# The exponentials of a banded attention, turned by transposing DMA transfers instead of TensorE and VectorE

## The chip, the cores and the metric

The kernel runs on one core of one Trainium2 chip. Five engines have their own instruction streams: TensorE (PE) multiplies and transposes into PSUM, VectorE (DVE) and ScalarE (ACT) work element by element, GpSimd (POOL) does so without access to PSUM and issues loads, SyncE (SP) issues transfers. Sixteen DMA engines carry out the transfers of all queues. The metric is device time in microseconds (us) of one execution, the median of several; lower is better.

## The reference

An attention over chunks of 32 tokens comes first: each chunk sees 16 tokens to the left, itself, 8 to the right, and 8 memory tokens, 64 in all. Then each token goes to two of eight experts. Cut to what matters:

```python
batch, n_heads, seq, head_dim = (4, 8, 768, 64)          # chunk, left, right = 32, 16, 8
for c in range(seq // chunk):
    k_full = concat([mem_k, k_ctx]); v_full = concat([mem_v, v_ctx])
    scores = scale * q_c @ k_full.T
    a = exp(scores - max(scores)); a = a / (sum(a) + 1e-09)
    out[:, :, c_start:c_end] = a @ v_full
x = out.transpose(0, 2, 1, 3).reshape(3072, 512)
noisy = x @ w_gate + log1p(exp(x @ w_noise)) * noise     # 8 experts, the best two are kept
for e in range(8):
    h = maximum(x[mask] @ w1[e], 0.0)                    # 512 -> 1024 -> 512
    out[mask] += top2_w[mask, k, None] * (h @ w2[e])
```

## The kernel before

The attention is a loop over 16 units (`NPAIR`), the expert part follows. Two units make up a group of four heads of one batch entry; a unit is one half of the 768 tokens of four heads: 3 tiles of 128 tokens (`UB`), 12 chunks. The instructions of each engine run in the order in which they are written (a manual schedule), and the loop (lines 591 to 648) interleaves several units by hand. For unit n:

- `qkT_pe` (L265): TensorE transposes q and k, ScalarE copies them out (L268, and L276 in `kT_act`), two to three units ahead.
- `scores_pe` (L290, L300, L305): scores of four heads and three tiles into one PSUM tile `ps_s`, of which there is one buffer. The 64 keys of a chunk are kept as even and odd halves of 32 columns.
- `max_dve` (L313), then `sub_dve`: VectorE subtracts the maximum (L318), ScalarE takes the exponential into `P` (L320), bf16, 128 tokens x 6 blocks x 128 columns, two buffers. A block is one tile and one half of the keys; its 128 columns are four heads x 32 keys.
- `PT_pe` (L327): six transposes by TensorE, one for each block, into the PSUM tile `p_p`. `PT_dve` (L332): one VectorE copy into `PT`, two buffers, in SBUF.
- `PV_pe`: the six products with the memory values and a column of ones (L341), then 24 with the values of the chunks (L345), both with `PT` as the stationary operand, into `ps_o`.
- `mult_dve`: VectorE takes the reciprocals (L357) and writes the normalised rows to `xrow` (L358).
- `xT_pe` (L369, copied out in L371): transposes of these rows for the router. After every fourth unit the router of a batch entry begins (`begin_route`, L549 on), and its small steps are spread over the next units by `early_steps` and `late_steps`.

In turn i of the loop the order is: transposes of P(i-1); maximum of i; transposes of q and k for a later unit; router steps; copy of PT(i-1); subtraction and exponential of i; PV(i-1); scores of i+1; more router steps; multiplication of i-1; `xT_pe` of i-2; loads. So on TensorE PV(i-1) stands ahead of the scores of i+1, and on VectorE the multiplication of i-1 ahead of the maximum of i+1. The last unit's P is turned behind the loop (lines 649 to 655).

Three PSUM buffers (`psT`, tag "tr") serve the transposes of q and k, of P and of the rows, and the router.

GpSimd's queue issues the loads of q, k, v and of the expert weights (L126, L134, L538, L543). SyncE's queue has few transfers in this stage: the memory values (L164) at the start, the router's weights (L209) and the noise (L215) in turns 3, 6 and 10, and `write_rows` (L548), which writes a batch entry's rows to memory in router step s4, in turns 8 and 12 for the first two batch entries and near or behind the end of the loop for the others. A transfer on this queue waits in order for what it needs.

Of the kernel before, what the change touches and what calls it, by code (L numbers as in the profile page):

```python
# [13 lines left out]
BF16 = mybir.dt.bfloat16  # L14
# [10 lines left out]
def kernel(  # L25
# [14 lines left out]
    nc = tc.nc  # L40
# [19 lines left out]
    NPAIR = B * HP  # L60
# [38 lines left out]
    def body():  # L99
        actx = ExitStack()  # L100
        ap_ = actx.enter_context(tc.tile_pool(name="ap", bufs=2))
# [61 lines left out]
        for hd in range(2 * GP):  # L163
            nc.sync.dma_start(  # L164
                out=mv_nat[QW * hd + WP:QW * hd + QW].rearrange("p g e d -> p g (e d)"),
                in_=bass.AP(mem_v.tensor, mem_v.offset + hd * n_mem * D, [[2 * D, n_mem // 2], [2 * GP * n_mem * D, NG], [1, 2 * D]]))
# [88 lines left out]
        st = [dict() for _ in range(NPAIR)]  # L255
# [22 lines left out]
        UB = BT // 2  # L278
# [29 lines left out]
        def bc4(ap, n):  # L308
            return ap.rearrange("p h (u o) -> p h u o", o=1).to_broadcast([128, 2, BT, n])
# [6 lines left out]
        def sub_dve(n):  # L316
            sd = ap_.tile([128, 2, BT, CTX], F32, name="sd")
            nc.vector.tensor_tensor(out=sd, in0=st[n]["ps"], in1=bc4(st[n]["mx"], CTX), op=Alu.subtract)  # L318
            P = ap_.tile([128, 2 * UB, 4, QW], BF16, name="P")
            nc.scalar.activation(out=P.rearrange("p x h c -> p h x c"), in_=sd.rearrange("p x (h u) (e c) -> p (x h) (u e) c", h=2, e=2), func=Act.Exp, scale=scale)  # L320
            st[n]["P"] = P

        def PT_pe(n):
            P = st[n]["P"]
            p_p = psT.tile([128, 2 * UB, 128], BF16, name="p_p", tag="tr")
            for x in range(2 * UB):
                nc.tensor.transpose(out=p_p[:, x, :], in_=P[:, x, :, :], identity=identb)  # L327
            st[n]["p_p"] = p_p

        def PT_dve(n):  # L330
            PT = ap_.tile([128, 2 * UB, 128], BF16, name="PT")
            nc.vector.tensor_copy(PT, st[n]["p_p"])  # L332
            st[n]["PT"] = PT

        def PV_pe(n):
            g, half = divmod(n, 2)
            PT, vg = st[n]["PT"], groups[g][2]
            po = psO.tile([128, UB, 512], F32, name="ps_o")
            for u in range(UB):
                for e in range(2):  # L340
                    nc.tensor.matmul(out=po[:, u, :OW], lhsT=PT[:, 2 * u + e, :], rhs=memv[:, g, e, :], start=(e == 0), stop=False, skip_group_check=True)  # L341
            for x in range(CB):
                u, r = divmod(x, 4)
                for e in range(2):
                    nc.tensor.matmul(out=po[32 * r:32 * r + 32, u, :MD], lhsT=PT[:, 2 * u + e, 32 * r:32 * r + 32],  # L345
                                     rhs=vg[:, CB * half + x, :, e, :], start=False, stop=(e == 1), skip_group_check=True)
# [244 lines left out]
        for i in range(NPAIR):  # L591
            if i >= 1:
                PT_pe(i - 1)
# [7 lines left out]
            if i >= 1:  # L601
                PT_dve(i - 1)
# [42 lines left out]
            if i == GP * (NG - 3) + 1:  # L645
                load_w1(0)
                load_w2(0)
                load_w1(1)
        n = NPAIR - 1
        PT_pe(n)  # L650
        PT_dve(n)
        xT_pe(n - 1)
        late_steps()
# [223 lines left out]
        for e in range(E):  # L877
# [38 lines left out]
            if e == E - 1:  # L916
# [3 lines left out]
                    out=out_part[NB], out_offset=bass.IndirectOffsetOnAxis(ap=s_si[:, 0:1], axis=0),  # L920
                    in_=spart[:, 0, :], in_offset=None, bounds_check=N - 1, oob_is_err=False)
# [11 lines left out]
    with tc.For_i(SPILL, end, 128) as i:  # L933
# [7 lines left out]
        for t in range(NP):  # L941
# [11 lines left out]
            out=xl, out_offset=None, in_=xd, in_offset=bass.IndirectOffsetOnAxis(ap=gi[:, 0:1], axis=0),  # L953
# [10 lines left out]
        with tc.For_i(0, E, 1) as e:  # L964
# [17 lines left out]
            out=out, out_offset=bass.IndirectOffsetOnAxis(ap=si[:, 0:1], axis=0),  # L982
            in_=o, in_offset=None, bounds_check=N - 1, oob_is_err=False)
# [30 lines left out]
```

## Time and profile before

| | us |
|---|---|
| time, median of 3 runs | 334.02 (332.93 to 334.89) |
| time of the profiled execution | 335.33 |
| its span | 333.7 |
| TensorE busy in the span | 288.1 (86%) |
| VectorE, ScalarE, GpSimd busy | 169.9, 133.4, 138.6 |
| first and last start of a unit's maximum (L313) | 14.7, 94.3 |
| granted TensorE clock, mean over the span | 0.957 |

A row of a group gives its line, engine and operation, what it writes and reads, how many instructions, busy time and mean length of one, and the idle time of the engine in front of them with what ended it. A row of a timeline gives start, length and the same names; in brackets stands the idle time in front of it and what ended it. "PEld" is TensorE's loading of the stationary operand. A row of one line's or one tile's instructions has the shortest, median and longest duration in ns, then the first and the last start. "SPq" is SyncE's sequencer: the length there is how long the issue held it, not how long the data took. Rows of DMA queues give packets, MB and the time of their packets as a share of sixteen engines' span; it passes 100% where an engine has several packets in hand.

### The profile page before, as it was taken

What the parts mean: (1) busy time and instruction counts of PE and PEld (TensorE: products, weight loads), DVE (VectorE), ACT (ScalarE), POOL (GpSimd) and SP (SyncE); (2) the same over time, 40 slices, a digit from 0 to 9 for tenths busy, and PEclk for the clock granted to TensorE, in tenths of its full rate; (3) what the DMA queues carried; (4) which work ended last, traced back from release to release, by engine and by line L of the source; (5) the groups of instructions that cost most, each with busy time, mean ns of one, the idle gap of its engine ahead of it and who ended that gap; (6) DMA issues with size and microseconds to landing.
All of it is one profiled execution on the core that took longest, in us unless ns stands there. A gap on an engine that the chain in (4) does not pass through costs nothing.

```text
span 333.7 us, 7301 instructions
## 1 busy us (share of the span) xinstructions
PE 288.1 (86%) x3019; PEld 173.5 (52%) x3019; DVE 169.9 (51%) x343; ACT 133.4 (40%) x235; POOL 138.6 (42%) x181
## 2 busy tenths in 40 slices
PE   1697887977776377999999999999999999999990
PEld 0575675755654256554754754544544544544540
DVE  7789859849958775222322323424342433434451
ACT  7877788757433033533333332332303303202200
POOL 7877868538023472781008007007152042042152
PEclk9999999979989559999999999999999999999997
DMA  7999999999997136699407905914959624521031
GB/s 99 179 163 176 184 163 163 210 143 101 214 225 216 23 88 93 128 156 238 87 0 125 221 4 110 223 28 105 207 147 166 117 111 70 86 109 60 1 140 71
DMA packets 58763, 42.99 MB, mean 129 GB/s; under 512 B 32449, under 2 KB 52033, under 8 KB 58728
## 3 DMA queue, kind: packets, MB, share of 16 engines
q0 software_dynamic: 49808, 38.71, 77.0%
q1 hardware_dynamic: 8632, 3.74, 5.6%
q8 instruction: 24, 0.39, 0.5%
q10 hardware_dynamic: 288, 0.07, 0.1%
q14 instruction: 11, 0.09, 0.1%
HBM read 61.23 MB, written 10.66 MB: 215 GB/s over the span
## 4 chain that ended last, share of the span: by engine, by line
PE 43%; issue 24%; DVE 13%; ACT 8%; POOL 7%; DMA 3%; POOLq 0%; DVEq 0%; ACTq 0%
PE ps_h L769 16%; PE ps_y L780 14%; POOL out_dram L788 4%; ACT kd L276 3%; PE ps_o L345 3%; DMA out_dram<-acc,sidx 2%; PE ps_o L341 2%; DVE mx L313 2%; DVE xrow L358 2%; DVE sd L318 2%; DVE vg L150 2%; PE p_t L705 2%; ACT xt L371 1%; ACT P L320 1%; PE p_t L265 1%
## 5 line engine op out<-in xcount | busy, mean ns | idle before, releaser
L769 PE MATMUL ps_h<-xTb,w1t 128*128 128x512 bf16 (+5 forms) x640 | 101.4, 320 | 1.5 <-DVE xTb L706 1.5
L780 PE MATMUL ps_y<-w2t,ht 128*128 128x512 bf16 x448 | 101.4, 379 | 0.0
L769 PEld LDWEIGHTS <-w1t 128*128 128x128 bf16 x640 | 58.6, 99 | 43.9 <-DVE xTb L706 1.1
L788 POOL DMA_INDIRECT out_dram<-acc,sidx x28 | 28.1, 1004 | 126.4 <-DVE acc L787 124.1
L756 DVE TENSOR_SCALAR ht<-ps_h 128x512 bf16<-128x512 f32 (+3 forms) x68 | 38.1, 560 | 68.1 <-PE ps_h L769 63.1
L780 PEld LDWEIGHTS <-ht 128*128 128x128 bf16 x448 | 42.9, 98 | 46.7
L754 ACT ACTIVATE ht<-ps_h 128x384 bf16<-128x384 f32 (+2 forms) x76 | 38.9, 511 | 70.4 <-PE ps_h L769 66.3
L784 ACT ACTIVATE acc<-ps_y,meta 128x512 f32<-128x512 f32 x28 | 19.2, 687 | 62.6 <-PE ps_y L780 45.4
L787 DVE SCALAR_TENSOR_TENSOR acc<-ps_y,meta,acc 128x512 f32<-128x512 f32 x28 | 21.0, 750 | 34.5 <-PE ps_y L780 34.5
L696 POOL DMA_INDIRECT xl<-x_rows,gidx x28 | 30.0, 1071 | 16.8 <-PE ps_h L769 6.6
L134 POOL DMA_DIRECT2D vg<-in_v_dram x34 | 25.5, 756 | 11.4 <-DMA kg<-in_k_dram 3.7
L706 DVE COPY xTb<-p_t 128x512 bf16<-128x512 bf16 x28 | 11.6, 422 | 28.6 <-PE p_t L705 28.4
L276 ACT COPY kd<-p_t 64x768 bf16<-64x768 bf16 x32 | 25.2, 786 | 1.0 <-PE p_t L265 0.8
L265 PE MATMUL p_t<-identb,qg 128*64 128x128 bf16 x192 | 10.3, 245 | 12.0 <-DMA qg<-in_q_dram 6.6
L371 ACT COPY xt<-p_x 128x768 bf16<-128x768 bf16 x16 | 12.8, 798 | 12.0 <-PE p_x L369 11.9
L341 PE MATMUL ps_o<-memv,PT 128*128 128x260 bf16 x96 | 15.0, 296 | 2.2 <-DVE PT L332 2.0
L320 ACT ACTIVATE P<-sd 128x768 bf16<-128x768 f32 x16 | 13.5, 845 | 8.1 <-DVE sd L318 8.1
L268 ACT COPY qT<-p_t 128x768 bf16<-128x768 bf16 x16 | 12.8, 800 | 8.9 <-PE p_t L265 8.8
L358 DVE TENSOR_TENSOR xrow<-ps_o,rec 128x768 bf16<-128x768 f32 x16 | 15.3, 958 | 0.6
L313 DVE TENSOR_REDUCE mx<-ps_s 128x12 f32<-128x768 f32 x16 | 15.1, 942 | 0.5 <-PE ps_s L300 0.5
L318 DVE TENSOR_TENSOR sd<-ps_s,mx 128x768 f32<-128x768 f32 x16 | 15.2, 949 | 0.0
L345 PE MATMUL ps_o<-vg,PT 128*32 128x256 bf16 x384 | 14.9, 293 | 0.0
(150 smaller groups left out, 287.5 us busy)
## 6 DMA issues: line engine op xcount, KB each, us to landing
w1t<-in_moe_w_dram POOLq DMA_DIRECT2D x8, 1024.0 KB, 11.4
w2t<-in_moe_w_dram POOLq DMA_DIRECT2D x8, 1024.0 KB, 10.1
vg<-in_v_dram POOLq DMA_DIRECT2D x30, 168.0 KB, 10.2
qg<-in_q_dram POOLq DMA_DIRECT2D x7, 384.0 KB, 9.9
kg<-in_k_dram POOLq DMA_DIRECT2D x7, 384.0 KB, 11.3
x_rows<-xrow SPq DMA_DIRECT2D x3, 792.0 KB
x_rows<-xrow SPq DMA_DIRECT2D x2, 384.0 KB
xl<-x_rows,gidx POOLq DMA_INDIRECT x28, 6.5
```

Source lines behind the costliest of these rows:

```text
L134: nc.gpsimd.dma_start(out=vg[p0 + j:p0 + j + nj, c:c + n, hd, :, :].rearrange("p c e d -> p c (e d)"), in_=bass.AP(v.tensor, v.offset + (g ...
L276: nc.scalar.copy(st[n]["kT"][hs, hh, :].rearrange("d (p j) -> d p j", j=SJ), st[n]["p_k"][hs].rearrange("d j p -> d p j"))
L313: nc.vector.tensor_reduce(out=mx, in_=st[n]["ps"], axis=AX, op=Alu.max)
L318: nc.vector.tensor_tensor(out=sd, in0=st[n]["ps"], in1=bc4(st[n]["mx"], CTX), op=Alu.subtract)
L345: nc.tensor.matmul(out=po[32 * r:32 * r + 32, u, :MD], lhsT=PT[:, 2 * u + e, 32 * r:32 * r + 32], rhs=vg[:, CB * half + x, :, e, :], start ...
L358: nc.vector.tensor_tensor(out=xr.rearrange("p u (h d) -> p u h d", d=D), in0=po[:, :, :MD].rearrange("p u (h d) -> p u h d", d=D), in1=rec ...
L696: nc.gpsimd.indirect_dma_start(out=xl, out_offset=None, in_=xd, in_offset=bass.IndirectOffsetOnAxis(ap=idx[:, p:p + 1], axis=0), bounds_ch ...
L754: nc.scalar.activation(out=dst, in_=src, func=Act.Relu)
L756: nc.vector.tensor_scalar(out=dst, in0=src, scalar1=0.0, scalar2=None, op0=Alu.max)
L769: nc.tensor.matmul(out=ps_h[:, o:o + w], lhsT=w1t[:, kp, f * 128:(f + 1) * 128], rhs=rhs(kp), start=(kp == 0 and i == 0), stop=(kp == KP - ...
L780: nc.tensor.matmul(out=ps_y, lhsT=ht[:, f, j * CAP:(j + 1) * CAP], rhs=w2t[:, f, :], start=(f == 0), stop=(f == FB - 1))
L788: nc.gpsimd.indirect_dma_start(out=out_part[p], out_offset=bass.IndirectOffsetOnAxis(ap=sidx[:, p:p + 1], axis=0), in_=a, in_offset=None, ...
```

## The change

For all units but the last, `PT_pe` allocates `PT` itself and issues six transposing transfers from `P` to `PT` on SyncE's queue, one for each block of 128 x 128 bf16 elements; TensorE's transposes and the PSUM tile are left out, and `PT_dve` does nothing. The last unit keeps the old way. The place in the written order is that of the call of `PT_pe`, at the head of the next turn.

```diff
         def PT_pe(n):
             P = st[n]["P"]
+            if n < NPAIR - 1:
+                PT = ap_.tile([128, 2 * UB, 128], BF16, name="PT")
+                for x in range(2 * UB):
+                    nc.sync.dma_start_transpose(out=PT[:, x, :], in_=P[:, x, :, :].rearrange("p h c -> p (h c)"))
+                st[n]["PT"] = PT
+                return
             p_p = psT.tile([128, 2 * UB, 128], BF16, name="p_p", tag="tr")
             for x in range(2 * UB):
                 nc.tensor.transpose(out=p_p[:, x, :], in_=P[:, x, :, :], identity=identb)
             st[n]["p_p"] = p_p
 
         def PT_dve(n):
+            if n < NPAIR - 1:
+                return
             PT = ap_.tile([128, 2 * UB, 128], BF16, name="PT")
             nc.vector.tensor_copy(PT, st[n]["p_p"])
             st[n]["PT"] = PT
```

## The prediction

> **What bounds the kernel now.** I read the span and windows by stage first, then the chain of waits inside the attention stage, then one turn of the loop in the timeline, and last the SyncE queue and the DMA queues, since that is where the change puts its work.
>
> Windows (length, busy time of each engine with its instructions, granted TensorE clock, DMA share, GB/s):
>
> ```profile
> core 0: us, PE busy (x) PEld busy (x) DVE busy (x) ACT busy (x) POOL busy (x), PEclk, DMA share, GB/s
> 14.00:104.00 90.00, 73.25 (x1645) 56.03 (x1636) 71.11 (x134) 59.70 (x86) 52.87 (x83) 0.96 1.58 173
> 119.00:334.00 215.00, 204.06 (x1214) 108.99 (x1212) 78.32 (x141) 60.58 (x130) 67.93 (x68) 0.98 0.53 111
> ```
>
> The first row is the attention stage, in which all of the change lies; the second is the expert stage, bound by TensorE (204 of 215 us) and left alone. In the attention stage no engine is full: TensorE 73, VectorE 71, ScalarE 60 of 90 us. The next view says what does bound it, the chain of waits inside 14 to 104 us, shares by line, largest first:
>
> ```profile
> by line: ACT kd L276 11.6%; PE ps_o L345 9.5%; issue 9.4%; PE ps_o L341 9.1%; DVE mx L313 6.8%; DVE xrow L358 6.4%; DVE sd L318 6.3%; ACT P L320 5.3%; PE p_t L265 5.0%; ACT qT L268 5.0%; ACT xt L371 4.5%; PE ps_s L300 3.2%; DVE PT L332 2.6%
> ```
>
> It hops through TensorE, VectorE and ScalarE: a loop of dependences across three engines, each in its written order. The pace of that loop is read from its first VectorE instruction, the row maximum of a unit, once per unit:
>
> ```profile
> L313 DVE TENSOR_REDUCE mx<-ps_s x16: 895/948/958, 14.7 to 94.3; 128x12 f32<-128x768 f32 x16
> ```
>
> Sixteen maxima, first start 14.7, last 94.3: (94.3 - 14.7) / 15 = 5.31 us a unit. One turn, in order of time (start, length):
>
> ```profile
> 82.27 0.83 PE L341 MATMUL ps_o<-memv,PT 128*128 128x260 bf16 x6
> 83.03 0.85 PE L345 MATMUL ps_o<-vg,PT 128*32 128x256 bf16 x24
> 83.95 0.23 DVE L357 RECIPROCAL rec<-ps_o 128x12 f32<-128x12 f32 x1
> 84.21 0.96 DVE L358 TENSOR_TENSOR xrow<-ps_o,rec 128x768 bf16<-128x768 f32 x1
> 85.09 0.95 DVE L313 TENSOR_REDUCE mx<-ps_s 128x12 f32<-128x768 f32 x1
> 85.95 0.55 DVE L332 COPY PT<-p_p 128x768 bf16<-128x768 bf16 x1
> 86.42 0.95 DVE L318 TENSOR_TENSOR sd<-ps_s,mx 128x768 f32<-128x768 f32 x1
> 87.46 0.84 ACT L320 ACTIVATE P<-sd 128x768 bf16<-128x768 f32 x1 [1.56 <-DVE sd L318]
> ```
>
> The reader is to see the closed path. The value products of unit i stand on TensorE ahead of the scores of unit i+2, and on VectorE the multiplication of unit i (L358) stands ahead of the maximum of unit i+2. So from PT(i) the path runs through L345, L358, L313, L318 to P(i+2), two units further; P(i+2) is then turned to PT(i+2), and the round begins again. One round takes two units. From the last of the L341 products (83.03) to the end of P (88.30) it is 5.27 us; without the copy of L332 between, which goes (86.42 - 85.95 = 0.47), 4.80; with some 0.2 for two hand-overs, 5.0 us. Now a round has 2 x 5.31 = 10.62 us, so the turn from P to PT may take **5.6 us** before the loop waits for it. This is the number that decides.
>
> **What goes.** For 15 of 16 units, six TensorE transposes and one VectorE copy (groups of the window 14 to 104):
>
> ```profile
> L327 PE MATMUL p_p<-identb,P 128*128 128x128 bf16 x96 | 8.8, 231 | 1.2 <-issue 1.1 <-ACT kd L276 0.2
> L332 DVE COPY PT<-p_p 128x768 bf16<-128x768 bf16 x16 | 8.8, 550 | 0.8 <-PE p_p L327 0.6
> ```
>
> That is 8.8 / 16 x 15 = 8.3 us of each engine. On the path lies much less: the chain has the copy at 2.6% of 90 = 2.3 us, and the transposes, not among its thirteen, at no more than that: together at most 4.7 us. That is the most the removal can give. A PSUM buffer of three also goes free; no row shows a wait for it worth a term, so I cost it at nothing (nothing but a small gain is possible).
>
> **What comes.** Ninety transfers, six a unit, each a 128 x 128 bf16 block (32 KB) from SBUF to SBUF, on SyncE's queue. No row shows a transposing transfer. Its price has two parts: how long SyncE is held by each (d), and how long after that the data has landed (f).
>
> For d the nearest rows are the transfers that this queue issues now:
>
> ```profile
> L548 SPq DMA_DIRECT2D x_rows<-xrow x6: 359/362/371, 58.8 to 111.2; - x6
> L215 SPq DMA_DIRECT2D nz_all<-in_moe_noise_dram x4: 665/1344/2292, 6.5 to 60.2; - x4
> ```
>
> Plain rows of 1 KB cost 0.36 us an issue, the noise, cut in pieces of 32 bytes, 0.67 to 2.29, median 1.34. A block whose every row is scattered over 128 partitions is nearer to the second than to the first: **d = 1.34 us**, with 0.36 and 2.29 as ends. Six in a row: 8.06 us (2.2 to 13.8).
>
> A page prices the operation: the Trainium skill, VectorE: DVE Perf Modes, section "The three transpose paths", gives 1309 ns for a 128 x 128 bf16 block by DMA crossbar against 390 ns by TensorE. By it six are 7.85 us and the forecast below would be about 3 us lower; it speaks against the change as the row does.
>
> For f there is one wait of this queue on its own small transfers (16 KB each):
>
> ```profile
> 2.18 1.39 SPq L164 DMA_DIRECT2D mv_nat<-in_mem_v_dram  x4
> 6.03 0.39 SPq L209 DMA_DIRECT2D wgn_f<-in_moe_w_noise_dram  x1
> SPq L209 <- DMA mv_nat<-in_mem_v_dram: 2.0, 1, 2.0
> ```
>
> Issued from 2.18 to 3.57, the wait ended at 6.03: f between 2.46 (the last) and about 3.5 (the first); I take 3.0. The upper end comes from the loads on the same engines, median us from issue to landing last:
>
> ```profile
> q0 software_dynamic: 32925, 13.25, 144.4%
> q1 hardware_dynamic: 4286, 2.09, 12.2%
> vg<-in_v_dram POOLq DMA_DIRECT2D x27, 168.0 KB, 9.8
> ```
>
> In this stage q0's packets alone overlap to 144% of all engines: each always has a load packet in hand. So f may rise to 9.8. The added 2.95 MB at q1's share (12.2% for 2.09 MB) would be 17% of 90 us, some 15 us of the engines. I cost that at nothing, because the loads run groups ahead and a slower loop asks for them later; were that cover gone, it would be the 15 us.
>
> **The waits and what stands behind them.** TensorE waits at L341 for the transfers. Behind it stand L345, the scores of the unit after next and the transposes of L369, so VectorE (L357, L313) and ScalarE (L371) wait too. SyncE itself now waits for P; behind it stand the next blocks and, in written order, the router's two weight loads, the four noise loads and two of the row writes, which so far found an idle queue. They are 4 x 1.34 + 2 x 0.39 + 2 x 0.36 = 6.9 us in front of blocks; half falls in time that is waited anyway, I take 3.5 (0 to 6.9). That a row write waits for its gates does not hold the blocks long: L463 to L466 run right behind the subtraction that P needs too.
>
> **TensorE's clock.** The row first:
>
> ```profile
> 91.00:97.00 6.00, 4.29 (x105) 3.35 (x103) 3.96 (x6) 2.08 (x5) 2.41 (x7) 0.99 1.19 232
> 97.00:103.00 6.00, 5.46 (x75) 3.59 (x74) 3.83 (x11) 2.58 (x4) 0.30 (x1) 0.72 0.97 213
> 96.47 1.09 PE L341 MATMUL ps_o<-memv,PT 128*128 128x260 bf16 x6 [0.65 <-DVE PT L332]
> 97.50 1.48 PE L345 MATMUL ps_o<-vg,PT 128*32 128x256 bf16 x24
> ```
>
> Around a stall in front of L341 the clock fell from 0.99 to 0.72, and L345 took 1.48 for 0.85. With several us of idle TensorE in every unit I expect such clocks for much of the stage: about +0.7 us a round (0 to 1.7, the whole of L341 and L345 once more).
>
> The Trainium skill, TensorE: Matmul & The Clock Gate, section "Why this matters for your kernels", asks for no idle gap over about 3 us between bursts, else the clock goes to half. By it L345's 0.85 doubles, and that instead of 0.7 makes about 1 us more in the whole stage. The trace agrees in the sign, at shorter gaps.
>
> **The sum.** A round is the turn (6d + f = 8.06 + 3.0 = 11.06) plus 5.0 plus 0.7 = 16.8 us for two units, 8.4 a unit; SyncE alone needs 6d = 8.06, so both bounds lie together and neither hides the other. 15 x (8.4 - 5.31) = 46.4 us, and 3.5 for the queue: 50 us. The profiled execution took 335.33 us (span 333.7), 1.31 above the median of 334.02, so 335.33 + 49.9 - 1.31 = **384 us**. The expert stage's 215 us stay.
>
> **Rivals.**
> (a) Slower, but by less: SyncE is held shortly, d at 0.67 as the fastest noise load. Then (4.0 + 2.5 + 5.0) / 2 = 5.8 us a unit, 15 x 0.45 = 7 us: 341; cases between here and the forecast fill 341 to 365. For it: a block has no 768 pieces. Against: TensorE's clock and the queue's own loads would add to it.
> (b) Starved by the loads: the engines hand each block's packets out between those of q0, and it lands like a vg load, f = 9.8. Round 8.06 + 9.8 + 5.7 = 23.6, 11.8 a unit, +97 us: 430. The same for d at its upper end: 13.8 a unit, +127 us, 460. For it: 144%. Against: q1's packets have had their turn so far, and a slower loop thins the loads.
> (c) Faster: the turn is hidden. At the row writes' 0.36 a block and f = 2.46 it takes 2.2 + 2.5 = 4.6 us, under the 5.6 that the loop allows; then only the removal counts, up to 4.7 us: 329. It decides from d below 0.52 us. Against: every cheap issue in the trace has long contiguous rows. The Trainium skill, Advanced Engine Details and Errata, section "X-Bar Transpose (TRN2)", says that transposing DMAs are as fast as ordinary ones, 350 to 400 GB/s; by that a block's data is an estimated 0.09 us and this rival would hold. No run shown here bears it out, and it speaks of bandwidth, not of issue or landing.
>
> **Chances.** Forecast (365 to 415) 0.60; (a) 0.15; (b) and what lies between, over 415, 0.18; (c) 0.05; within 0.5% 0.02, where the turn just fits. 0.5% (1.7 us) is about what a measurement here tells from no change. Range: 346 to 436, which cuts some 0.1 at the low end and 0.1 at the high one. Faster 0.05, same 0.02, slower 0.93; the likeliest case's own range is 365 to 415.
>
> **What will show it.** SyncE's transposing issues should last near 1.34 us and stand almost back to back; the maxima of L313 should come every 8.4 us; TensorE's wait at L341 should name a DMA into PT; the clock should be below 0.96 in the stage; the expert stage should keep its 215 us. I am wrong if issues last about 0.4 us (then a or c), if they end early but L341 still waits long after (then b), or if loads of q and k are what TensorE waits for.

## The result, and the profile after

| | us |
|---|---|
| before, median of 4 runs | 334.05 (332.93 to 334.89) |
| after, median of 4 runs | 408.47 (408.12 to 411.32) |
| after / before | 1.225 (95%: 1.218 to 1.232) |
| profiled execution after: time, span | 408.40, 406.8 |

The change made the kernel 74 us slower. Of some kernels in the next section, single executions took over 1.5% longer than the fastest of the same kernel; the ratios there leave these out, the medians do not (two of e9's four), and e2, e8 and e11 were profiled in one. The new lines in `PT_pe` and `PT_dve` push what stands below them down by 8: the products are now L349 (memory values) and L353 (values of the chunks), the reciprocals L365, the multiplication L366; the transfers are L328.

The windows of the kernel after, the attention stage and the expert stage (columns as before):

```profile
core 0: us, PE busy (x) PEld busy (x) DVE busy (x) ACT busy (x) POOL busy (x), PEclk, DMA share, GB/s
14.00:180.00 166.00, 87.12 (x1588) 57.95 (x1580) 67.93 (x131) 60.50 (x90) 54.37 (x88) 0.76 1.07 116
195.00:407.00 212.00, 201.78 (x1201) 106.99 (x1199) 75.54 (x138) 59.85 (x128) 65.42 (x66) 0.98 0.54 112
```

VectorE and ScalarE are busy about as long as before (68 and 60 us, before 71 and 60), but in 166 us in place of 90; the expert stage is nearly the same. The chain of waits in the attention stage, by line, and one row for the maxima, one for the transfers' hold on SyncE, one for the wait of the products:

```profile
by line: DMA PT<-P 30.2%; SPq L328 26.2%; DMA x_rows<-xrow 8.2%; PE ps_o L353 6.6%; ACT P L320 3.6%; DVE sd L318 2.9%; DVE xrow L366 2.9%; PE ps_o L349 2.7%; DVE mx L313 2.6%; issue 2.0%; PE p_x L377 2.0%; ACT kd L276 1.8%; PE ps_l L388 1.1
```

```profile
L313 DVE TENSOR_REDUCE mx<-ps_s x16: 895/947/952, 14.7 to 163.4; 128x12 f32<-128x768 f32 x16
L328 SPq DMA_TRANSPOSE PT<-P x90: 1094/1232/2275, 17.5 to 167.9; - x90
```

```profile
L349 PE MATMUL ps_o<-memv,PT 128*128 128x260 bf16 x96 | 25.9, 340 | 75.3 <-DMA PT<-P 75.1
```

The loop over three engines has gone from the top of the chain. In its place stand the transfers, in two parts: SyncE held by issues (26% of 166 us = 43 us) and data that has not landed yet (30%, 50 us). TensorE sits 75 us in front of L349. The pace of the loop is (163.4 - 14.7) / 15 = 9.91 us a unit against 5.31: 15 x 4.60 = 69 us of the 73.1 us by which the span grew (406.8 - 333.7). The other 4 us lie behind the last maximum: 406.8 - 163.4 = 243.4 against 333.7 - 94.3 = 239.4.

How a round runs, from the timeline of the kernel after (TensorE's rows of L349 with what ended their wait, SyncE's transfers, ScalarE's exponentials):

```profile
101.00 0.85 ACT L320 ACTIVATE P<-sd 128x768 bf16<-128x768 f32 x1
101.73 0.37 SPq L556 DMA_DIRECT2D x_rows<-xrow  x1
102.21 16.87 SPq L328 DMA_TRANSPOSE PT<-P  x12
106.59 0.84 ACT L320 ACTIVATE P<-sd 128x768 bf16<-128x768 f32 x1 [0.51 <-ACT qT L268]
109.07 0.40 PE L349 MATMUL ps_o<-memv,PT 128*128 128x260 bf16 x1 [2.63 <-DMA PT<-P]
111.59 0.40 PE L349 MATMUL ps_o<-memv,PT 128*128 128x260 bf16 x1 [2.12 <-DMA PT<-P]
113.49 1.09 PE L349 MATMUL ps_o<-memv,PT 128*128 128x260 bf16 x3 [1.50 <-DMA PT<-P]
120.86 0.84 ACT L320 ACTIVATE P<-sd 128x768 bf16<-128x768 f32 x1
```

The units go in pairs. P of unit 8 is done at 101.85 and P of unit 9 only 5.6 us later, while SyncE still issues the blocks of unit 8; it goes on with those of unit 9 without a gap, twelve transfers at 16.87 / 12 = 1.41 us each. The next P (unit 10) comes at 121.70, 19.85 us after that of unit 8: two units in one round, as the prediction had the loop. The blocks of unit 8 arrive two us and more apart at first, slower than they are issued.

### The profile page after: what moved, and what is told of

The parts are those of the page before. It is cut to its first block, busy times and chain, and to the rows that moved or that the text cites. A ratio compares the mean times of both kernels' runs of the same rounds, so it can differ in the third digit from the quotient of the medians.

```text
span 406.8 us, 7271 instructions
## 1 busy us (share of the span) xinstructions
PE 300.2 (74%) x2929; PEld 173.7 (43%) x2929; DVE 164.3 (40%) x328; ACT 133.0 (33%) x235; POOL 138.4 (34%) x181
## 4 chain that ended last, share of the span: by engine, by line
PE 56%; DMA 17%; SPq 11%; DVE 9%; ACT 3%; issue 2%; POOL 0%; POOLq 0%; DVEq 0%; ACTq 0%
PE ps_h L777 25%; PE ps_y L788 23%; DMA PT<-P 12%; SPq L328 11%; DMA x_rows<-xrow 3%; PE ps_o L353 3%; ACT P L320 1%; PE p_t L713 1%; DVE vg L150 1%; DVE sd L318 1%; DVE xrow L366 1%; PE ps_o L349 1%; DVE mx L313 1%; PE p_x L377 1%; ACT kd L276 1%
## 5 line engine op out<-in xcount | busy, mean ns | idle before, releaser
L349 PE MATMUL ps_o<-memv,PT 128*128 128x260 bf16 x96 | 25.9, 340 | 75.3 <-DMA PT<-P 75.1
L349 PEld LDWEIGHTS <-PT 128*128 128x128 bf16 x96 | 9.4, 103 | 89.5 <-DMA PT<-P 87.3
L365 DVE RECIPROCAL rec<-ps_o 128x12 f32<-128x12 f32 x16 | 3.7, 233 | 93.8 <-PE ps_o L353 93.8
L415 POOL TENSOR_TENSOR nl<-ns,nz_all 128x48 f32<-128x48 f32 x3 | 0.9, 286 | 55.9 <-ACT lg L407 55.9
L353 PE MATMUL ps_o<-vg,PT 128*32 128x256 bf16 x384 | 18.8, 347 | 0.0
L318 DVE TENSOR_TENSOR sd<-ps_s,mx 128x768 f32<-128x768 f32 x16 | 15.3, 958 | 1.2
## 6 DMA issues: line engine op xcount, KB each, us to landing
w1t<-in_moe_w_dram POOLq DMA_DIRECT2D x8, 1024.0 KB, 11.9
```

## The experiments

Each kernel is the changed one with one edit, unless another is named. The ratios are to the kernel before on the same chip and the same job, since chips differ by over 1% (before: 333.4, 333.6 and 338.7 us in the three jobs).

| | median us | ratio to before (95%) |
|---|---|---|
| e1, one transfer a unit | 378.9 | 1.133 (1.126 to 1.140) |
| e2, plain copies, six a unit | 380.2 (376.9 and 383.5) | |
| e3, row writes on ScalarE's queue | 408.3 | 1.222 (1.216 to 1.228) |
| e4, few loads | 396.5 | 1.188 (1.181 to 1.196) |
| e5, one transfer, few loads | 359.1 | 1.077 (1.070 to 1.084) |
| e6, before, few loads | 329.1 | 0.987 (0.981 to 0.993) |
| e7, TensorE kept busy | 419.4 | 1.257 (1.250 to 1.263) |
| e8, one transfer, products one turn later | 372.1 | 1.113 (1.106 to 1.120) |
| e9, one transfer, row writes on ScalarE's queue | 381.5 | 1.114 (1.106 to 1.122) |
| e10, one transfer, late weights | 378.1 | 1.115 (1.109 to 1.121) |
| e11, e8 with late weights | 368.6 | 1.086 (1.079 to 1.093) |
| e12, before, late weights | 347.1 | 1.025 (1.020 to 1.029) |

**e1: is it the number of issues?**

```diff
-                for x in range(2 * UB):
-                    nc.sync.dma_start_transpose(out=PT[:, x, :], in_=P[:, x, :, :].rearrange("p h c -> p (h c)"))
+                nc.sync.dma_start_transpose(out=PT, in_=P.rearrange("p x h c -> p (x h c)"))
```

> The six transposing transfers of a unit become one transfer of 128 x 768 elements; same bytes, same place, one issue. Theory (the pace is half of: issues of a unit x 1.23 us, plus landing, plus 5.7 us of the rest of the round): with one issue of about 1.3 us and a landing of 3 to 7 us the maxima come every 5.0 to 7.0 us, the time is 335 to 365 us. Rival A (the crossbar's work on the bytes sets it, however it is cut): SyncE is held, or the data lands, about 7 us or more after the start; pace 8 us or more, time over 380 us. Rival B (starved by the loads): landing stays near 7 us in the stretch with loads, falls behind it; time 355 to 385 us.

378.9 us: 30 us less than after, so the issues carry a good part, but above what the theory said and within rival B's span. The hold on SyncE and two rows of the timeline, kernel e1:

```profile
L327 SPq DMA_TRANSPOSE PT<-P x15: 1211/1340/5335, 17.5 to 139.2; - x15
```

```profile
26.32 1.48 PE L348 MATMUL ps_o<-memv,PT 128*128 128x260 bf16 x6 [7.13 <-DMA PT<-P]
113.30 0.37 SPq L555 DMA_DIRECT2D x_rows<-xrow  x1
132.14 1.48 PE L348 MATMUL ps_o<-memv,PT 128*128 128x260 bf16 x6 [12.22 <-DMA PT<-P]
```

One transfer of six blocks holds SyncE 1.34 us, about as long as one block does (1.23): the hold goes by the instruction, not by its bytes. But P of unit 0, done at 17.5, has landed only at 26.3; and unit 12, whose row write was issued at 113.30 just ahead of its transfer, waited until 132.1. Landing is long and uneven. A pace of (140.5 - 14.7) / 15 = 8.4 us (maxima below) and such a landing would fit rival A too; e2 and e5 decide on it.

**e2: is it the transposing?**

```diff
-    NEG = -1e30
+    NEG = 0.0
...
-                    nc.sync.dma_start_transpose(out=PT[:, x, :], in_=...)
+                    nc.sync.dma_start(out=PT[:, x, :], in_=...)
```

> The six transfers of a unit become plain copies of the same blocks to the same places, so P isn't transposed and the values are others; the mask of the missing context is left out too (its constant is 0), so that no sum is zero. Theory: an issue costs 0.36 us as for other plain rows, so the turn shrinks by 6 x 0.87 = 5.2 us, the pace by at least 2.6 us a unit, to about 6.5 to 7.3; time 355 to 370 us. Rival B (the loads and row writes on the same engines set the landing): the landing stays, the time is above 390 us. Rival A (the transposing crossbar itself is slow): the time falls below 350 us, since issue and landing shrink both.

380.2 us, between the theory's 370 and rival B's 390. The hold, kernel e2:

```profile
L328 SPq DMA_DIRECT2D PT<-P x90: 464/600/3030, 17.5 to 143.1; - x90
```

A plain copy of a block holds SyncE 0.60 us, not the 0.36 of the row writes; a transposing one twice as long. Six plain copies a unit are as slow as one transposing transfer, so what is left above the kernel before does not need the transposing. Rival A, which asked for less than 350 us, is out; that the landing makes the rest is tested by e4 and e5.

**e3: do the row writes on the same queue cost anything?**

```diff
-            nc.sync.dma_start(out=xd_part[view]..., in_=xrows[b][:, t:z, lo:hi])
+            eng = nc.scalar if view < 2 else nc.sync
+            eng.dma_start(out=xd_part[view]..., in_=xrows[b][:, t:z, lo:hi])
```

> The row writes of the first two batch entries (792 KB each) are issued on ScalarE's queue instead of SyncE's, at the same place in the written order. Theory (the transposing transfers of the next unit wait behind these writes in the same queue's rings): the two slow turns, 11.4 and 14 us at 102 to 116 and 140 to 155 us, shrink to the others' length; the chain's 8.4% of 161 us = 13.5 us goes, time 393 to 400 us. Rival (what counts is that both need the same sixteen engines): the turns stay long, time 404 to 410 us.

408.3 us, no gain, against the theory and as its rival had it. The chain's 8.2% for `x_rows`, a single wait of 13.6 us, was not won back. With six issues a unit the queue of these writes costs nothing that shows; e9 asks again with one.

**e4, e5, e6: do the loads cost it?** Groups 3 to 7 use the tiles of three groups before, and their loads of q, k and v are left out.

```diff
         def new_group(g):
+            if g >= 3:
+                groups[g] = groups[g - 3]
+                return
...
         def load_qk(g, i=None):
+            if g >= 3:
+                return
...
         def load_v(g):
+            if g >= 3:
+                return
```

> The changed kernel without the loads of q, k and v of groups 3 to 7: these use the tiles of three groups before again, so values of 5 of 8 groups are others. Theory: the landing is long only because the engines are full of load packets; without them from about 30 us on it falls to some 1.2 us as in the quiet end, the turn is 6 x 1.23 + 1.2 = 8.6 us, the pace (8.6 + 5.7) / 2 = 7.2 us; with two row writes left the time is 370 to 385 us. Rival C (the landing does not depend on the loads): 400 us or more. If the loads were all of it, the time would be below 350 us.

> One transfer a unit as in e1, and the loads of q, k and v of groups 3 to 7 left out as in e4 (values of 5 of 8 groups are others). Theory now: two costs that cover each other, the issues (6 x 1.38 = 8.3 us a unit, which is the whole pace of e4 in its quiet stretch) and the landing beside the loads (which is the pace of e1). With both gone the turn is some 1.3 + 3 us and the pace comes back to 5 to 6 us; time 335 to 352 us (some turns beside the weight loads stay long). Rival (the crossbar's work on a unit's 196 KB takes 7 us by itself): the pace stays near 8 us as in e1, time 370 us or more.

> Control: the kernel before without the loads of q, k and v of groups 3 to 7 (values of 5 of 8 groups are others). Both theories: nothing there waited for these loads, so 330 to 337 us. If it were much faster, e4 and e5 would have to be read against it.

e4: 396.5 us, 12 less than after, not the 24 to 38 expected. SyncE's timeline of e4, three units, then two, in the stretch without loads:

```profile
47.52 25.25 SPq L335 DMA_TRANSPOSE PT<-P  x18
73.50 16.58 SPq L335 DMA_TRANSPOSE PT<-P  x12
```

25.25 / 18 = 1.40 and 16.58 / 12 = 1.38 us a transfer with no gap: SyncE is the bound, 6 x 1.39 = 8.3 us a unit. The expectation had used half the round and forgotten that SyncE alone is slower than that. The landing itself did shrink as the theory said. With the DMA engines nearly idle, the last product of unit 4 starts at 65.08, its sixth issue having ended at 63.94:

```profile
47.50:91.00 43.50, 29.86 (x527) 19.61 (x527) 19.69 (x37) 21.96 (x32) 4.34 (x14) 0.75 0.16 26
65.08 0.40 PE L356 MATMUL ps_o<-memv,PT 128*128 128x260 bf16 x1 [0.87 <-DMA PT<-P]
```

From the end of a unit's sixth issue to the start of its last product it is 1.1 to 1.3 us in each of the units 3 to 10 of e4. In the kernel after it is 3.6 to 8.5 us in units 0, 2, ... 12, and 1.15 in unit 14, behind the loads. In e4 too it is long beside the loads that stayed: 5.6 in unit 0, 7.6 in unit 12 beside the weights. So the loads make the landing long. Taking them away left SyncE's issues as the bound: two costs of about the same size cover each other, and removing one shows little.

e5 takes both away: 359.1 us; the control e6 is 329.1, so the loads alone are worth 4 us. Maxima of e5 at the ends of its quiet stretch (units 5 and 13), and a turn in it:

```profile
48.88 0.95 DVE L320 TENSOR_REDUCE mx<-ps_s 128x12 f32<-128x768 f32 x1
91.25 0.95 DVE L320 TENSOR_REDUCE mx<-ps_s 128x12 f32<-128x768 f32 x1
57.66 0.84 ACT L327 ACTIVATE P<-sd 128x768 bf16<-128x768 f32 x1
62.22 0.85 PE L355 MATMUL ps_o<-memv,PT 128*128 128x260 bf16 x6 [1.61 <-DMA PT<-P]
```

Eight units in 42.37 us: 5.30 a unit. P of unit 6 is done at 58.50, the whole PT is there at 62.22: 3.7 us, and 4.5 to the products of L359, the point up to which the prediction's 5.6 was counted. Counted that way, units 5 to 11 take 3.6 to 7.6 us, 5.0 in the mean; two of them, 8 and 9, at a row write, lie above 5.6. So with one issue and idle engines the turn all but hides, as rival (c) had it. Maxima of the same two units in the control e6, then in the kernel before:

```profile
38.57 0.95 DVE L320 TENSOR_REDUCE mx<-ps_s 128x12 f32<-128x768 f32 x1
79.35 0.95 DVE L320 TENSOR_REDUCE mx<-ps_s 128x12 f32<-128x768 f32 x1
```

```profile
39.15 0.95 DVE L313 TENSOR_REDUCE mx<-ps_s 128x12 f32<-128x768 f32 x1
85.09 0.95 DVE L313 TENSOR_REDUCE mx<-ps_s 128x12 f32<-128x768 f32 x1
```

That is (79.35 - 38.57) / 8 = 5.10 a unit with the same loads left out, and (85.09 - 39.15) / 8 = 5.74 in the kernel before with its loads. So with the turn all but hidden the pace is still 0.2 us a unit behind the control, and no gain shows from the work taken off TensorE and VectorE. What e5 loses, it loses beside loads that stayed, above all here (kernel e5):

```profile
90.09 13.36 SPq L334 DMA_TRANSPOSE PT<-P  x2
110.03 1.48 PE L355 MATMUL ps_o<-memv,PT 128*128 128x260 bf16 x6 [18.81 <-DMA PT<-P]
```

Twenty us for one transfer, where 3 MB of expert weights and a row write of 792 KB had just been issued.

**e7: the clock.** In `PT_dve`, for the 15 units:

```diff
             if n < NPAIR - 1:
+                fill = psT.tile([128, 2 * UB, 128], BF16, name="fill", tag="tr")
+                for x in range(60):
+                    nc.tensor.transpose(out=fill[:, x % 6, :], in_=identb, identity=identb)
                 return
```

> The changed kernel with 60 TensorE transposes of the identity in each of the 15 units, written just ahead of the router steps' copy place (before the value products), so that TensorE works instead of waiting; their results go nowhere. Theory: the granted clock of the stage rises from 0.76 towards 1, the value products shorten by some 0.6 to 0.9 us a round, time 2 to 8 us less: 400 to 406 us. Rival (the clock has no part in it): 407 us or more, since the fill can only delay.

419.4 us, slower. Its attention stage:

```profile
14.00:180.00 166.00, 119.92 (x2331) 99.57 (x2320) 59.62 (x107) 56.65 (x82) 52.04 (x81) 0.86 1.27 110
```

The clock did rise, 0.76 to 0.86, but the 60 transposes stand in front of the products also where the data had landed, which may cost more than the clock gives. The run does not tell what the clock is worth; that stays open but for the rows in the next section.

**e8: is it latency or work?** One transfer a unit, and the products, all that follows them and the loads of v one turn of the loop later; P and PT have three buffers. The main lines of it:

```diff
-            if i >= 1:
-                PV_pe(i - 1)
+            if i >= 2:
+                PV_pe(i - 2)
...
-                mult_dve(i - 1)
+                mult_dve(i - 2)
...
-                xT_pe(i - 2)
+                xT_pe(i - 3)
```

> One transfer a unit as in e1, and the value products, the multiplication, the transposes for the router, the router's begin and the loads of v stand one turn of the loop later; P and PT have three buffers, sd one. Theory (the turn's latency is what costs, not work): three units share one round, pace (L + 5.7) / 3 with L the 8 to 13 us of e1's turn is 4.6 to 6.2 us; with 3 us more at the end, 335 to 352 us. Rival (the engines' bandwidth beside the loads is used up by the transposes): the pace stays above 7 us, time over 362 us.

372.1 us, 7 less than e1, outside the theory's range and in its rival's, at a pace of 6.7 us. The turns of units 13 and 14, beside the weights, take 28 and 27 us from P to the products of the chunks (the 30 in e11's expectation is too long). The chain of e8 from 14 to 140 us, and the landing of its loads of v:

```profile
by line: DMA PT<-P 35.6%; DMA vg<-in_v_dram 14.8%; DMA kg<-in_k_dram 14.0%; PE ps_o L348 7.6%; PE ps_o L352 5.3%; POOL vg L134 3.0%; issue 2.8%; POOL memv L200 2.6%; PE p_t L265 2.3%; DVE sd L318 1.5%; DVE xrow L365 1.5%; ACT P L320 1.3%; D
```

```profile
vg<-in_v_dram POOLq DMA_DIRECT2D x27, 168.0 KB, 15.8
```

With more room for the transfers the loads of v and k come onto the chain; in the chains of before and after they are not among the listed lines. These loads also land later: 15.8 us in the median for v, against 9.8 in the kernel before and 8.0 in e1. So it is not latency alone: the transfers land late beside the loads (e4), and beside the transfers of e8 the loads land late. How much of the second comes from e8's later issue of the loads of v is not shown.

**e9 to e12: row writes or weights?** e9 is e1 with e3's edit. e10 is e1, e11 is e8, and e12 is the kernel before, each with the weight loads in the last turn:

```diff
-            if i == GP * (NG - 3) + 1:
+            if i == NPAIR - 1:
                 load_w1(0)
```

> One transfer a unit as in e1, and the row writes of the first two batch entries on ScalarE's queue as in e3. In e1 the turn of unit 12 takes 20.3 us; 792 KB of rows stand in front of its transfer on the queue, and 3 MB of expert weights are on the engines. Theory R (the rows in front of it in the same queue make the wait): the turn falls under 12 us, the time to 366 to 372 us. Theory W (the weight loads make it): it stays over 15 us and the time at 376 to 381 us.

> One transfer a unit as in e1, and the three loads of expert weights that stand in turn 11 stand in the last turn, 15. Theory W (the weight loads make the turns of units 12 and 13 long): these turns fall from 20 and 16 us to about 8, the time by 10 to 20 us to 360 to 368 us, if the expert stage does not wait for the weights. Theory R (the rows in front): 374 us or more.

> Value products one turn later as in e8, and the weight loads in the last turn as in e10. In e8 the turn of unit 14 took 30 us beside the weights. Theory W: it falls to about 10, the time to 348 to 358 us; what stays over the kernel before is the wait of loads and transfers for each other (e8's pace of 6.7 us against 5.3) and 3 us at the end. Rival: the weights are then waited for in the expert stage, time over 365 us.

> Control for e10 and e11: the kernel before with the weight loads in the last turn. Both theories: no wait for these loads in the attention stage, so 330 to 338 us; over 340 us would mean that the expert stage waits for the weights, and e10 and e11 would have to be read against that.

The maxima of e1, e9 and e10, in this order, a view of each:

```profile
L313 DVE TENSOR_REDUCE mx<-ps_s x16: 895/947/958, 14.7 to 140.5; 128x12 f32<-128x768 f32 x16
```

```profile
L313 DVE TENSOR_REDUCE mx<-ps_s x16: 895/948/952, 14.7 to 132.5; 128x12 f32<-128x768 f32 x16
```

```profile
L313 DVE TENSOR_REDUCE mx<-ps_s x16: 895/947/951, 14.7 to 125.0; 128x12 f32<-128x768 f32 x16
```

Both theories hold a part. With the row writes in another queue (e9) the ratio falls from 1.133 to 1.114, with intervals that do not touch, though e9's rests on two executions; its median is no lower than e1's because that chip is slower. The last maximum comes 8.0 us earlier, but 4.1 of these were there at the maximum of unit 8 already (78.93 against 83.02), before the first row write was issued, so some 4 us are left for the queue. The turn of unit 12, from P to the products of the chunks, is 14.8 us against 20.2: between the two theories. With the weights later (e10) the last maximum comes 15.5 us earlier. Unit 12 of e10, with the row write still in front:

```profile
110.48 0.84 ACT L320 ACTIVATE P<-sd 128x768 bf16<-128x768 f32 x1 [0.59 <-DVE sd L318]
111.30 0.37 SPq L555 DMA_DIRECT2D x_rows<-xrow  x1
116.81 1.51 PE L348 MATMUL ps_o<-memv,PT 128*128 128x260 bf16 x6
```

5.5 us from P to the first product, where e1 needed 18.8. But e10's ratio of 1.115 is only 0.018 (6 us) below e1's: the control e12 shows that the later weights alone cost 2.5%, 8.4 us, and GpSimd's first gather of e10's expert stage stood idle for 12 us, as it did in e12 (11.8; 2.8 in the kernel before):

```profile
152.01 1.19 POOL L703 DMA_INDIRECT xl<-x_rows,gidx  x1 [12.00 <-issue]
```

15.5 - 8.4 = 7 us, about what the ratios show. e11, with both, is the best of the DMA kernels that keep all loads and still 8.6% (7.9 to 9.3) slower than before. Its expected 348 to 358 us was missed; its rival's over 365 us came, and there too that first gather stood idle for 11.9 us. None of the kernels with the transposing transfers beats the kernel before.

## Why the prediction was right, and where not

The direction and the bound were right, and 408.47 lies in the stated range and in the forecast case's own (365 to 415). The time was forecast 24 us too low, so it lies near the upper end of that range. Of the span's 73.1 us, 69 came from the pace, where 46.4 were forecast, and 4 from the end, where none were; 3.5 forecast for the queue did not show. Step by step:

**The loop.** That one round takes two units and closes over L353, L366, L313, L318 and L320 held, and so did its length without the turn. Two rounds of the kernel after, from its timeline:

```profile
96.18 1.48 PE L353 MATMUL ps_o<-vg,PT 128*32 128x256 bf16 x24
101.00 0.85 ACT L320 ACTIVATE P<-sd 128x768 bf16<-128x768 f32 x1
102.51 0.85 PE L353 MATMUL ps_o<-vg,PT 128*32 128x256 bf16 x24
106.59 0.84 ACT L320 ACTIVATE P<-sd 128x768 bf16<-128x768 f32 x1 [0.51 <-ACT qT L268]
```

From the start of L353 to the end of P: 101.85 - 96.18 = 5.67 us in the first, where L353 took 1.48, and 107.43 - 102.51 = 4.92 in the second, where it took 0.85. Predicted were 5.0, and 0.7 more where the clock has fallen. Over all rounds it is 6.0 us in the mean from units 0, 2, ... 12 and 5.0 from units 1, 3, ... 13; the longest, 7.2, is the one from 114.50 to 121.70, where the router's steps stood on ScalarE ahead of the exponential.

**The hold of SyncE.** Forecast 1.34 us an issue, taken from the noise loads; measured 1.23, and 1.38 to 1.40 from one to the next when nothing else holds it. Six are 8.3 us against 8.06. Right, and a bound by itself, as e4 shows. The Trainium skill's 1309 ns (VectorE: DVE Perf Modes, "The three transpose paths") lies between the two measured figures. The remark in the prediction that it makes the forecast about 3 us lower holds for SyncE as the bound; by the sum, which halves the turn, it is 15 x 0.21 / 2 = 1.6 us.

**The landing is the term that was mis-sized.** The prediction took f = 3.0 us, the wait of small transfers at the start, and put the landing beside the loads (9.8) into a rival with the rest left at the forecast. Two units in 19.82 us (2 x 9.91) less 5.7 leave some 14 us for the turn, of which 8.3 are the issues: f was near 6 us, twice what was taken; (8.3 + 6 + 5.7) / 2 = 10. Read unit by unit from the trace it comes out the same: along units 0, 2, ... 12, whose blocks find the queue free or nearly so, it is in the mean 8.3 us from the first issue to the end of the sixth, 5.7 more to the start of the last product of L349, 0.3 to L353 and 6.0 to the next P, together 20.3 of a round of 20.4, (160.7 - 17.5) / 7 from P of unit 0 to P of unit 14. (The 19.82 is lower because the first two units start only 3.4 us apart.) The blocks of the odd units, but for unit 13, stand 3.2 to 5.4 us behind those of the even unit on the queue; the prediction did not name this wait, but it does not lengthen the round, which closes over the even units. The landing was longest, 8.5 us, in unit 4, and 1.15 in unit 14; the windows of both, kernel after, with DMA shares of 1.96 and 0.09:

```profile
62.00:78.00 16.00, 5.42 (x72) 2.88 (x73) 1.69 (x8) 3.88 (x6) 4.35 (x6) 0.58 1.96 138
158.00:174.00 16.00, 9.09 (x139) 5.69 (x135) 6.24 (x11) 4.50 (x8) 2.41 (x7) 0.79 0.09 17
```

With one transfer and few loads it is short: PT was there 3.7 us after P, the issue included (e5, unit 6). Beside the loads it took 8.8 us (e1, unit 0), beside weights and row write 20 us (e5). So the forecast and rival (b) were not two cases but two ends of one, and the truth lay between them.

**The queue.** 3.5 us were set for the transfers in front of the blocks. With six issues a unit the row writes cost nothing that e3 could show; with one they cost some 4 to 6 us (e9 against e1).

**The clock.** Forecast below 0.96, it was 0.76 over the stage. What it costs in time was only read off single rounds (5.67 against 4.92); e7 could not isolate it.

**What was taken away.** At most 4.7 us were allowed for it. In the one stretch where the turn was all but hidden (e5) the pace was 5.30, and the control's 5.10 over the same units was not reached; so a gain from the 8.3 us of TensorE and VectorE was not seen anywhere. That transposing goes as fast as ordinary transfers (the Trainium skill, Advanced Engine Details and Errata, "X-Bar Transpose (TRN2)") did not decide: six plain copies a unit were 28 us faster than six transposing transfers (e2 against after), with a shorter hold on SyncE, and no faster than one transposing transfer (e1). A block's cost here was its issue and its wait; no run measures the bandwidth.

**The end.** The 4 us behind the last maximum were not in the sum. The last of the turned units (14) lands there, in front of the last products.

Left open: what makes a small transfer land so late beside loads. The runs show that it does, for plain copies too, and that it falls when loads, weights or row writes go; they do not show what happens inside the DMA engines. What the lower clock costs in the whole stage is open too.

## What to carry to other kernels

Before work is moved from a half-idle engine to a DMA queue, find the round of dependences that it stands in and how long its step may take there; here 5.6 us, of which the kernel before used 3.3 in the mean from P to PT, about 1.1 of it work of TensorE and VectorE, and the kernel after some 14 for issues and landing. Price a step on a queue as issues times hold plus landing, and take the landing from transfers in the same stretch, among the same loads, not from a quiet one. When two costs cover each other, as issue and landing did, removing one shows little: remove both, with a control.

## What the runs showed of the hardware that was not expected

- A transposing transfer held SyncE 1.23 us for 32 KB and 1.34 us for 196 KB (medians, after and e1): one transfer of six blocks costs SyncE about one hold in place of six.
- A plain copy of a 32 KB block from SBUF to SBUF held it 0.60 us, the 792 KB row write 0.37.
- The same transfer of 196 KB landed 3.7 us after its data was ready in a quiet stretch and 20 us after beside 3 MB of weights and a row write (e5).
- The last block of a unit landed 1.1 to 1.3 us after its issue ended with the DMA engines nearly idle (e4, units 3 to 10) and 3.6 to 8.5 us after beside the loads (after, units 0, 2, ... 12).
- More room for the transfers (e8) brought waits for the loads of k and v onto the chain, 14.0 and 14.8%, where the kernel before had none among its listed lines; the loads of v landed in 15.8 us in place of 9.8.
